# Four small moves in the program order of an FFT and MLP kernel: stage 4 behind the second product, a matrix load split elsewhere, one spectrum a step sooner, no product between two evictions

## The chip, the cores and the metric

The kernel runs on one core of a Trainium2 chip. The metric is the device time of one execution in microseconds (us), and smaller is better.

Short names: PE is the tensor engine, DVE the vector engine, ACT the scalar engine, POOL the GpSimd engine, SP the engine whose queue issues most transfers. L305 is line 305 of the kernel.

## The reference, cut to what matters

```python
def _attn_ref(x, filt_r, filt_i):                  # x: 8 x 3136 x 256
    X = np.fft.rfft(x, axis=1)
    F = (filt_r + 1j * filt_i)[None, :, :]
    return np.fft.irfft(X * F, n=x.shape[1], axis=1)

def _moe_ref(x, U, V, w_ch1, w_ch2):               # takes the result above as x
    xt = x.transpose(0, 2, 1)
    h = xt @ U @ V                                 # rank 32 over the sequence
    u = x + h.transpose(0, 2, 1)
    ch = np.maximum(u @ w_ch1, 0.0) @ w_ch2        # 256 -> 1024 -> 256
    return u + ch
```

The sequence of 3136 is transformed as 64 x 49, so the Fourier part is a row of small matrix products: stages 1 and 2 forward, a product with the filter, stages 3 and 4 back.

## The kernel before: the parts that matter

The program order of every engine is written by hand. For each of the 8 images:

- stage 1 (L305) into PSUM bank 4, copied out by ACT or DVE (`asb`, L309) and stored to memory (L313); its last rows are a tile of their own, `al`, stored at L297;
- stage 2 (L400) from the reloaded tiles `a` (L363) into banks 5 and 6; the filter products on DVE (L727 to L731) or POOL;
- stage 3 (L392) into bank 7, copied out by ACT (`esb`, L370) and stored (L377);
- stage 4 (L589) from the reloaded tiles `e` (L549) and the constant matrix `sv` into bank 4 again, evicted by DVE into `ut` (L594).

Then come the first product (L600, banks 0 and 1, with relu on ACT into `hring`, L604) and the second (L633, banks 2 and 3), the residual (L609), an eviction to `och` (L641) and the output store (L648).

The work on 512 tokens is a group. There are 52 groups of 8 steps, 416 steps with one relu each. I write (n, t) for step t of group n. The main loop:

```python
of = {"m": (0, 1), "o": (2, 3), "w": (4,), "e": (7,), ... "u": (5, 6)}[tag]   # PSUM banks by use

def st1(b, by=()):
    tag = "u" if b == 1 else "w"          # stage 1 of images 2 and up: bank 4, as stage 4

for n, gr in enumerate(groups):
    for t in range(8):
        for f, a in early[8 * n + t]:     # DVE and POOL products of the filter
            f(*a)
        mm1(gr, t)                        # first product, relu
        turns = {0: (5, 6), 5: (6, 7), 12: (6, 7)}.get(n, (2, 6))
        if n + 1 < len(groups) and t in turns:
            stage4(groups[n + 1], turns.index(t))       # one half of the next group's stage 4
        if n:
            mm2_part(groups[n - 1], t)    # second product of the group before
        for f, a in plan[8 * n + t]:      # stages 1 to 3, loads, stores
            f(*a)
```

So every step is a first product, perhaps a half of stage 4, a second product, and perhaps some piece of stages 1 to 3 of a later image.

## Time and profile before

| | us |
|---|---|
| median of 3 runs | 557.28 (556.37 to 560.54) |
| span in the profiled run | 553.0, mean granted clock 0.996 |
| PE waits for the copy of stage 1's result (L589 <- ACT asb) | 4.4 in 13 places |
| PE waits for the matrix `sv` | 2.2 in 1 place |
| PE waits for L594's eviction (L589 and L600 <- DVE ut) | 1.9 and 1.4 |
| PE waits for `e` of image 1 (L589 <- DMA e) | 1.2 in 1 place |

PE is busy for 93% of the span, so what can be won is the sum of its short idle times. A row of waits says who released PE. It does not say that PE would have been sooner without that wait, because another one may stand right behind it. The lines themselves are in the prediction.

### The profile page before, as it was taken

How to read it: one execution, taken by the hardware profiler on the slowest of the kernel's cores; microseconds unless marked ns; L12 is line 12 of the kernel's file. 1: busy time of each engine (PE TensorE's matmuls, PEld its weight loads, DVE VectorE, ACT ScalarE, POOL GpSimd, SP SyncE). 2: the span in 40 equal slices, each digit the busy share in tenths (PEclk: the TensorE clock that was granted, in tenths of full speed). 3: DMA queues.
4: the chain of work that ended last, by engine and by line, in shares of the span. 5: the costliest groups of instructions: out<-in, count | busy, mean ns of one | idle time of the engine just before them, and what ended most of it. 6: DMA issues, size and time to landing. Idle time of an engine off the chain costs nothing.

```text
span 553.0 us, 11722 instructions
## 1 busy us (share of the span) xinstructions
PE 516.4 (93%) x4540; PEld 371.9 (67%) x4540; DVE 353.8 (64%) x410; ACT 374.3 (68%) x677; POOL 291.6 (53%) x208
## 2 busy tenths in 40 slices
PE   5897789988989899999999999999999999999996
PEld 2644557666666576767776777777786777777775
DVE  7984747565456955768746775768646887543332
ACT  4655467746876578777777788668767677765663
POOL 6755277989873664834683185807563287300000
PEclk9999999999999899999999999999999999999999
DMA  9999895669663976974879459865654554343212
GB/s 195 166 194 188 197 221 152 173 189 232 167 184 104 211 198 150 234 214 120 195 204 215 128 168 243 164 202 152 181 163 131 140 161 121 107 113 115 96 77 86
DMA packets 85287, 91.96 MB, mean 166 GB/s; under 512 B 6725, under 2 KB 69464, under 8 KB 85232
## 3 DMA queue, kind: packets, MB, share of 16 engines
q1 hardware_dynamic: 67616, 75.02, 46.5%
q0 software_dynamic: 16912, 15.74, 18.7%
q8 instruction: 35, 0.57, 0.5%
q10 hardware_dynamic: 704, 0.46, 0.3%
q14 instruction: 20, 0.16, 0.1%
HBM read 57.12 MB, written 49.77 MB: 193 GB/s over the span
## 4 chain that ended last, share of the span: by engine, by line
PE 68%; DVE 9%; POOL 7%; DMA 5%; ACT 4%; issue 2%; SPq 0%; POOLq 0%; ACTq 0%; DVEq 0%
PE psum L633 24%; PE psum L600 23%; PE psum L400 5%; PE psum L392 4%; PE psum L589 4%; PE psum L609 3%; DMA x<-in_x_dram 2%; PE psum L305 2%; POOL fc L409 2%; DVE tb L729 2%; DVE tb L731 2%; POOL y L733 2%; ACT asb L309 1%; DVE ut L594 1%; DVE och L641 1%
## 5 line engine op out<-in xcount | busy, mean ns | idle before, releaser
L604 ACT ACTIVATE hring<-psum 128x512 f16<-128x512 f32 (+1 forms) x416 | 238.2, 576 | 113.4 <-PE psum L600 111.9
L600 PE MATMUL psum<-ut,w1sb 128*128 128x512 f16 (+1 forms) x832 | 240.3, 369 | 1.9 <-DVE ut L594 1.4
L633 PE MATMUL psum<-w2sb,hring 128*128 128x256 f16 x1536 | 230.7, 273 | 0.0
L733 POOL TENSOR_TENSOR y<-ta,tb 113x1024 f16<-113x1024 f16 x52 | 112.0, 2158 | 140.0 <-DVE tb L731 105.0
L633 PEld LDWEIGHTS <-hring 128*128 128x128 f16 x1536 | 143.0, 98 | 63.2 <-issue 3.0
L594 DVE CAST ut<-psum 128x512 f16<-128x512 f32 x94 | 69.6, 741 | 106.3 <-PE psum L589 81.3
L600 PEld LDWEIGHTS <-w1sb 128*128 128x128 f16 x832 | 104.4, 145 | 21.9 <-issue 5.5
L641 DVE COPY och<-psum 128x512 f32<-128x512 f32 x96 | 66.1, 689 | 50.2 <-PE psum L609 49.3
L370 ACT CAST esb<-psum 98x512 f16<-98x512 f32 x128 | 75.1, 587 | 25.4 <-PE psum L392 20.1
L589 PEld LDWEIGHTS <-e 96*128 96x128 f16 x752 | 34.5, 97 | 31.4 <-issue 11.9
L609 PE MATMUL psum<-idn,ut 128*128 128x128 f16 x392 | 54.1, 220 | 0.0
L309 ACT CAST asb<-psum 128x512 f16<-128x512 f32 x76 | 44.9, 590 | 13.3 <-PE psum L305 12.1
L727 DVE TENSOR_TENSOR ta<-psum,fb 113x1024 f16<-113x1024 f32 x37 | 45.0, 1217 | 6.2 <-PE psum L400 5.7
L589 PE MATMUL psum<-sv,e 96*128 96x64 f16 x752 | 37.4, 193 | 11.3 <-ACT asb L309 4.4
L729 DVE TENSOR_TENSOR tb<-psum,fc 49x1024 f16<-49x1024 f32 x37 | 45.4, 1226 | 1.0
L731 DVE TENSOR_TENSOR tb<-psum,fc 49x1024 f16<-49x1024 f32 x37 | 45.1, 1218 | 1.0
L609 PEld LDWEIGHTS <-ut 128*128 128x128 f16 x392 | 38.4, 98 | 4.9
L400 PE MATMUL psum<-a,w2t 98*128 98x512 f16 x120 | 36.2, 378 | 5.4 <-DVE tb L731 2.5
L727 POOL TENSOR_TENSOR ta<-pc,fb 113x1024 f16<-113x1024 f16 x15 | 32.4, 2161 | 13.4 <-ACT pc L737 13.4
L392 PE MATMUL psum<-y,g 113*98 113x512 f16 x98 | 37.6, 384 | 1.8 <-POOL y L733 0.9
L305 PE MATMUL psum<-x,wf 128*128 128x256 f16 x168 | 31.8, 272 | 3.2 <-DMA x<-in_x_dram 2.6
L187 POOL DMA_DIRECT2D x<-in_x_dram x48 | 31.0, 663 | 4.5 <-DMA w1sb<-in_moe_w_ch_dram 2.4
(112 smaller groups left out, 393.1 us busy)
## 6 DMA issues: line engine op xcount, KB each, us to landing
out_dram<-och SPq DMA_DIRECT2D x47, 512.0 KB
ct<-esb SPq DMA_DIRECT2D x64, 196.0 KB
x<-in_x_dram POOLq DMA_DIRECT2D x48, 256.0 KB, 7.6
e<-ct SPq DMA_DIRECT2D x46, 256.0 KB
a<-ct SPq DMA_DIRECT2D x56, 196.0 KB
ct<-asb SPq DMA_DIRECT2D x42, 256.0 KB
w1sb<-in_moe_w_ch_dram POOLq DMA_DIRECT2D x1, 512.0 KB, 6.6
w2sb<-in_moe_w_ch_dram POOLq DMA_DIRECT2D x1, 512.0 KB, 8.8
```

What stands on the lines that cost most here:

```text
L370: nc.scalar.copy(esb[b, k][:, 2 * half:2 * half + 2, :].rearrange("p s d -> p (s d)"), pe[0:98])
L392: nc.tensor.matmul(pe[0:98], g3[0:NZ, m, :], v, start=(n == 0), stop=(n == len(parts) - 1))
L400: nc.tensor.matmul(pz, w, a, start=True, stop=True)
L589: nc.tensor.matmul(pu[:, 64 * i:64 * i + 64], e2[b, c][:, i, 128 * dh:128 * dh + 128], sv[:, 64 * r:64 * r + 64], start=(i == 0), stop=Tru ...
L594: (nc.scalar.copy if gr is groups[0] and dh else nc.vector.tensor_copy)(o, v)
L600: nc.tensor.matmul(ph[:, 0:n], w1sb[:, dh, :, t], gr.ut[:, dh, 0:n], start=(dh == 0), stop=(dh == 1))
L604: nc.scalar.activation(h[:, 0:n], ph[:, 0:n], RELU)
L609: nc.tensor.matmul(o[:, dh * 128:dh * 128 + 128], gr.ut[:, dh, t0:t0 + n], idn, start=False, stop=(dh == 1), skip_group_check=True)
L633: nc.tensor.matmul(o, gr.h[tt][:, i * 128:(i + 1) * 128], w2sb[:, tt, :], start=(tt == 0), stop=False, skip_group_check=True)
L641: nc.vector.tensor_copy(gr.och[:, 2 * y:2 * y + 2, :].rearrange("p j d -> p (j d)"), gr.pc)
L727: eng.tensor_mul(ta, p[0:NZ], va)
L733: nc.gpsimd.tensor_add(ys[k], ta, tb)
```

## The change

It has four parts, each aimed at one of the rows above.

1. Where the step before ran a piece of stage 1 in bank 4, stage 4 goes behind the second product, which fills the time of the copy.
2. `sv` is split at column 1536 instead of 1024, so that stage 4 of blocks 0 to 2 needs only the first load.
3. The last two halves of stage 3 of image 1, and with them the loads of `e` for image 1 and its low-rank part, move up one step.
4. In groups 5 and 12 the DVE product that stood between the evictions of the two halves of stage 4 goes elsewhere.

```diff
-                    nc.sync.dma_start(sv[0:64, 0:1024], s4_d[:, 0:1024])
+                    nc.sync.dma_start(sv[0:64, 0:1536], s4_d[:, 0:1536])        # part 2
     def ok_dve(s):
-        return s % 8 not in (2, 6) and not small(s) and not small(s + 2)
+        return s % 8 not in ((6, 7) if s // 8 in (5, 12) else (2, 6)) and ...   # part 4 (cut)
-                    at(q + (3 if k == 7 else 2), three_q, k, half)
-            return 40
+                    at(q + 2, three_q, k, half)                                 # part 3
+            return 39
-    at(5, lambda: nc.sync.dma_start(sv[0:64, 1024:], s4_d[:, 1024:]))
+    at(5, lambda: nc.sync.dma_start(sv[0:64, 1536:], s4_d[:, 1536:]))           # part 2
-            if n + 1 < len(groups) and t in turns:
-                stage4(groups[n + 1], turns.index(t))
-            if n:
-                mm2_part(groups[n - 1], t)
+            behind = any(f is step1 for f, _ in plan[8 * n + t - 1])            # part 1
+            for side in (False, True):
+                if n + 1 < len(groups) and t in turns and behind == side:
+                    stage4(groups[n + 1], turns.index(t))
+                if n and not side:
+                    mm2_part(groups[n - 1], t)
```

More of the change, by code (lines that the diff above doesn't have):

```diff
@@ L696, in ok_dve @@
     def ok_dve(s):
-        return s % 8 not in (2, 6) and not small(s) and not small(s + 2)
+        return s % 8 not in ((6, 7) if s // 8 in (5, 12) else (2, 6)) and not small(s) and not small(s + 2)
     def step_at(w):
```

## The prediction

> **What bounds the kernel now.** I read the page first, then the waits of the tensor engine (PE), the timeline around each wait, the chain that ended last, and the windows of 20 us. From the page:
>
> ```profile
> PE 516.4 (93%) x4540; PEld 371.9 (67%) x4540; DVE 353.8 (64%) x410; ACT 374.3 (68%) x677; POOL 291.6 (53%) x208
> ...
> PE 68%; DVE 9%; POOL 7%; DMA 5%; ACT 4%; issue 2%; SPq 0%; POOLq 0%; ACTq 0%; DVEq 0%
> ```
>
> PE is the bound over the whole span, and from about 260 us on it is busy for 95 to 100% of nearly every window: little is to be won there, and whatever is won before is carried to the end. The waits of PE are short:
>
> ```profile
> PE psum L589 <- ACT asb L309: 4.4, 13, 0.7
> ...
> PE psum L589 <- DMA sv<-s: 2.2, 1, 2.2
> PE psum L589 <- DVE ut L594: 1.9, 1, 1.9
> ...
> PE psum L600 <- DVE ut L594: 1.4, 4, 0.4
> ...
> PE psum L589 <- DMA e<-ct: 1.2, 1, 1.2
> ```
>
> Columns: total us, times, longest. L589 is stage 4, L309 the copy of stage 1's result out of PSUM, L600 the first product. Each part of the change aims at one of these rows. The first row in the PE timeline (start, duration, idle in brackets):
>
> ```profile
> 85.31 0.38 PE L305 MATMUL psum<-x,wf 128*128 128x256 f16 x2
> 85.52 0.59 PE L600 MATMUL psum<-ut,w1sb 128*128 128x512 f16 x2
> 86.36 0.39 PE L589 MATMUL psum<-sv,e 96*128 96x64 f16 x8 [0.24 <-ACT asb L309]
> 86.59 0.60 PE L633 MATMUL psum<-w2sb,hring 128*128 128x256 f16 x4
> ```
>
> Stage 1 (L305) fills PSUM bank 4, ACT copies it out (0.59 us), stage 4 wants the same bank. The idle time in brackets understates the loss, since a busy bar holds the pipeline's tail too: two first products otherwise follow each other at 0.435 us, so stage 4 could have started at 85.52+0.435 = 85.955. It started 0.405 us later.
>
> Two stretches where PE is not what sets the pace. POOL and the load of x for image 3:
>
> ```profile
> 118.14 1.03 POOL L412 COPY fb<-fb 49x1024 f16<-49x1024 f16 x1
> 119.24 0.74 POOL L414 COPY fb<-fc 1x256 f16<-1x256 f16 x1
> 120.04 0.64 POOL L416 MEMSET fc<- 1x256 f16 x2
> 121.67 0.18 POOL L185 COPY x<-hring 1x1 f16<-1x1 f16 x1 [0.99 <-ACT hring L604]
> ```
>
> The chain that ended last runs over POOL without a break from 96.6 to 120.7 us, then the x load, and at 131.22 PE waits 0.44 us for that load. And DVE, where one product (L731) stands between the evictions of stage 4's two halves:
>
> ```profile
> 188.83 0.72 DVE L594 CAST ut<-psum 128x512 f16<-128x512 f32 x1
> 189.59 0.68 DVE L556 COPY e<-h 32x2048 f16<-32x2048 f16 x1
> 190.30 1.22 DVE L731 TENSOR_TENSOR tb<-psum,fc 49x1024 f16<-49x1024 f32 x1
> 191.55 0.73 DVE L594 CAST ut<-psum 128x512 f16<-128x512 f32 x1
> ```
>
> **What the Trainium skill says.** "TensorE: Matmul & The Clock Gate", section "Step-by-step: what each phase is for": matmuls stay in program order and only weight loads are pulled ahead. So products that do not need bank 4 can't pass a waiting stage 4 by themselves; the order in the program decides. The trace agrees: L633 follows L589 in every such place, though its inputs are old. "PSUM — Partial Sum Buffer", "PSUM bank collisions raise a hardware error": two engines may not touch a bank at once, so the wait for the copy can be filled but not dropped; here PE never starts before the 0.59 us copy ends. "DMA: Bandwidth & Descriptors", "Anatomy of one DMA": a fixed cost of about 2.0 us per transfer, mostly the receipt of the write. The trace agrees roughly: the last spectrum store of image 1 is issued at 110.44 (0.55 long) and the load that needs it follows at 113.53, 2.5 us later.
>
> **Part 1: stage 4 behind the second product.** By the order of the two programs 14 real halves move (groups 2, 3, 4, 7, 8, 10, 13, 14, 15). Their losses, each worked out as above, are 0.67, 0.41, 0.41, 0.42, 0.41 (80 to 106 us); 0.67, 0.40, 0.42, 0.82 (134 to 163 us); 0.40, 0.41, 0.71, 0.41, 0.40 (200 to 224 us): 6.9 us. Four L633 take 0.435 us, so each place gives at most 0.435: 5.8 us in sum. But stage 4 itself starts no sooner (it still waits for the copy), and so the eviction of stage 4 and the DVE products behind it come no sooner against stage 1. Where a stage 2 (L400) soon waits for those products, PE only waits there instead:
> - 80.5 and 86.4 count (0.84); 92.0 is lost, as the product before the L400 at 96.61 ends at 96.48, only 0.1 us of slack.
> - 98.1 and 105.6 count (0.82), up to the x load.
> - 134.0 is lost at the L400 at 138.44, which already waits 0.58 for DVE; of 139.9 and 146.0 some 0.38 is left at the L400 at 151.23; 162.5 is lost at the L400 at 166.25, which already waits 1.28.
> - 200.9 to 223.6: DVE has slack (for instance it ends 206.3 before an L400 at 207.5), all five count: 0.40+0.41+0.44+0.41+0.40 = 2.04.
>
> **Part 2: the stage-4 matrix in need's order.** Stage 4 of block 2 at 61.36 waits for the second part of sv, of which it reads the first 512 columns. Those now come with the first part, issued near 26 us. PE's loss is 61.36-(58.51+0.435) = 2.4 us. But its weight load waits for e until 60.68 (an idle of 2.02 us put down to DMA e). So the wait turns into one for e, and 0.6 us is won, not 2.4.
>
> **Part 3: spectrum 1 a step sooner.** The last two stage-3 halves, the load of e for image 1 and its low-rank part move up one step. Stage 4 at 117.39 waits 1.22 us (1.38 of issue) for that load. I expect the wait gone: with the SP queue in its new order the store goes out 1.5 to 2 us sooner. Two things take it back. First, the store of stage 1's last rows (al) now stands behind both e loads in the SP queue, and the load of the first spectrum block of image 2 waits for it: store about 112.5, landed some 2.5 us later, load 2.8 to 3.5 us, so at about 118.5 on the old scale while PE would be at its L400 (119.39 before) at 117.2. I expect a new wait of about 1 us there. Second, the x load for image 3 waits for POOL, which ends at 120.68 on the old scale. It was issued at 121.67, waiting for group 6's first relu. That relu can come sooner, the load by at most 0.97 us. So of 0.82+1.38+0.49 (the last is the wait at L600 at 120.54) only 0.97 arrives at 131.22.
>
> **Part 4: no product between the halves, groups 5 and 12.** In group 12 DVE's product of 1.23 us moves behind the second eviction. The first product's second half started at 192.34, could start at 191.62: 0.72 us. The wait of 1.9 us at 189.61 stays, because the products ahead of the first eviction stay. In group 5 no product stood between; nothing.
>
> **Sum:** before 96.6 us 0.6+0.84 = 1.45; to 131 us 0.97; to 166 us 0.38; at 192 us 0.72; to 224 us 2.04. Together 5.56 us of 557.28, which gives 551.7; I say 552.0.
>
> **Rivals.** (a) All PE losses named are won in full: 5.8 (part 1) + 2.4 + 1.4 + 0.7 + 0.5 = 10.8 us, 546.5. For it: PE carries 68% of the chain. Against it: DVE's waits at L400 (2.5 us in the waits) and the POOL stretch in the chain. (b) Nearly nothing comes through: the x load is not sooner because DMA is busy (shares of 0.93 to 0.95 in the windows around 60 to 80 and 120 to 140 us), stage 4 behind the products delays evictions and stage 1 waits for the bank in turn; 1 to 2 us, 555.5. Against it: the stretch from 200 to 224 us has slack on all engines. (c) Something turns worse: the delayed load of image 2's first block stalls PE by 3 us or more and pushes the later chain; 557 to 559. Against it: the x load wait behind it has room for 1 to 2 us. (d) The clock: from 190 to 193 us the windows show a granted clock of 0.50, behind the idle of 1.9 us. "TensorE: Matmul & The Clock Gate", "HAM oscillation — how this bites in real kernels", ties such drops to idle gaps of over about 3.4 us; this gap was shorter, so the trace does not quite agree. If new gaps move such a drop in or out, that is worth about 1.5 us either way.
>
> **Range and chances.** Terms of about 1 us are uncertain each (e's landing, the x load, the clock, the spread of the three runs from 556.4 to 560.5). I take 549.0 to 555.5. Faster by over 2% needs under 546.1, more than rival (a): 0.05. Slower by over 2% needs 568: 0.01. Within 2%: 0.94.
>
> **What would show it.** Right: the row L589 <- ACT asb falls from 4.4 us to under 1; L589 <- DMA sv gone and a wait for e of 1 to 2 us at the same place; L589 <- DMA e at 117 gone; L305 <- DMA x at 131 longer than 0.44, or a new L400 <- DMA a near 117; L400 <- DVE tb above 2.5. The gain by 131 us should be about 2.4 us and from 193 to 230 us about 2. Wrong: no new wait for x or a (then rival a is nearer), or L305 waiting for DVE ut in many steps (rival b).

## The result, and the profile after

The changed kernel took 551.04 us in the median of 4 runs (550.45 to 551.65), against 558.52 of 4 runs of the kernel before beside it (556.37 to 560.54). The ratio is 0.9867, with a 95% interval of 0.9822 to 0.9911: within 2%. Ratios here are the mean time of one kernel's fast runs over that of the other's of the same rounds, so not quite the ratio of the medians. In a later session the same kernel took 550.64 us against 555.12 (ratio 0.9905, 0.987 to 0.994). So the four runs of the kernel before in the first comparison lay at the high end of its spread, and some 5 us is the better figure for the gain: the mean of all 10 runs of the changed kernel is 550.8, that of 44 runs of the kernel before in four sessions 556.0.

The page of the changed kernel, busy time and chain:

```profile
PE 517.8 (94%) x4540; PEld 373.8 (68%) x4540; DVE 353.3 (64%) x410; ACT 374.1 (68%) x677; POOL 292.4 (53%) x208
...
PE 73%; DVE 9%; DMA 8%; POOL 4%; ACT 3%; issue 2%; SPq 0%; DVEq 0%; POOLq 0%; ACTq 0%
```

The same instructions and the same busy times, as it must be where only the order changes. In the chain PE has gone from 68 to 73% and POOL from 7 to 4%, but the transfers (DMA) from 5 to 8%: something new waits for a transfer. The waits of PE in the changed kernel (total us, times, longest):

```profile
PE psum L589 <- DMA e<-ct: 3.7, 3, 1.8
PE psum L400 <- DVE tb L731: 3.1, 4, 1.4
...
PE psum L589 <- DVE ut L594: 1.9, 1, 1.9
...
PE psum L392 <- ACT esb L370: 1.4, 3, 0.7
...
PE psum L600 <- DVE ut L594: 0.7, 2, 0.4
PE psum L400 <- DMA a<-ct: 0.7, 1, 0.7
...
PE psum L589 <- ACT asb L309: 0.5, 1, 0.5
```

The row of the copy fell from 4.4 us in 13 places to 0.5 in one. The row of `sv` is gone, and L600 <- DVE ut halved. But the wait for `e` grew from 1.2 us in one place to 3.7 in three, and L400 <- DMA a is new. What part 1 did is plain in the PE timeline, at the place that the prediction showed at 85.31 to 86.59:

```profile
84.95 0.59 PE L600 MATMUL psum<-ut,w1sb 128*128 128x512 f16 x2
85.38 0.60 PE L633 MATMUL psum<-w2sb,hring 128*128 128x256 f16 x4
85.82 0.40 PE L589 MATMUL psum<-sv,e 96*128 96x64 f16 x8
```

L600 and L633 follow each other at 0.43 us, then L589 at 0.44, with no idle. Before, L589 came 0.84 us behind L600.

To see which part won what, I cut each trace at the starts of the relus (one per step, so the same 416 marks in every kernel). Durations in us; "x late" marks where PE waited for the load of x for image 3, "w" a window of half clock, both explained below:

| kernel | (1,0) to (2,0) | (2,0) to (4,4) | (4,4) to (7,0) | (7,0) to (7,4) | (7,4) to (12,4) | (12,4) to (13,4) | (13,4) to (17,0) | (17,0) to the last relu |
|---|---|---|---|---|---|---|---|---|
| before | 11.21 | 33.53 | 28.24 | 6.53 x late | 48.33 | 12.93 w | 37.92 | 311.90 |
| before, again | 11.12 | 33.53 | 28.25 | 7.11 x late | 48.34 | 14.21 w | 37.91 | 311.93 |
| changed | 10.76 | 32.25 | 29.50 | 5.51 | 48.29 | 12.71 w | 36.19 | 311.91 |
| changed, again | 10.56 | 32.25 | 29.18 | 5.51 | 48.29 | 11.31 | 36.20 | 311.88 |
| part 1 alone | 13.07 w | 32.25 | 28.19 | 5.51 | 48.31 | 12.93 w | 36.28 | 311.90 |
| part 3 alone | 13.54 w | 33.53 | 29.44 | 5.92 | 48.33 | 14.82 w | 37.92 | 311.90 |
| parts 1, 2, 4 | 12.91 w | 32.24 | 28.19 | 6.36 x late | 48.29 | 11.31 | 36.20 | 311.91 |

Stretches without a mark, in kernels that have the same parts there, repeat within 0.1 us, except the first one and, with part 3, the one from (4,4), which repeat within 0.2 to 0.4 (the first one took 12.00 in experiment 7, where the wait for `sv` was 3.0 us instead of 2.2). That is much finer than the times of whole runs. Two places got better by over a microsecond, (2,0) to (4,4) and (13,4) to (17,0), and one got worse, (4,4) to (7,0). There image 1 takes over from image 0: part 3's place.

### The profile page after: what moved, and what is told of

Read it like the earlier page. It is cut to its first block, busy times and chain, and to the rows that moved or that the text cites. A ratio compares the mean times of both kernels' runs of the same rounds, so it can differ in the third digit from the quotient of the medians.

```text
span 549.9 us, 11727 instructions
## 1 busy us (share of the span) xinstructions
PE 517.8 (94%) x4540; PEld 373.8 (68%) x4540; DVE 353.3 (64%) x410; ACT 374.1 (68%) x677; POOL 292.4 (53%) x208
## 4 chain that ended last, share of the span: by engine, by line
PE 73%; DVE 9%; DMA 8%; POOL 4%; ACT 3%; issue 2%; SPq 0%; DVEq 0%; POOLq 0%; ACTq 0%
PE psum L633 26%; PE psum L600 25%; PE psum L400 5%; PE psum L392 4%; PE psum L589 4%; PE psum L609 3%; DMA e<-ct 3%; DMA x<-in_x_dram 3%; PE psum L305 3%; DVE tb L729 2%; DVE tb L731 2%; ACT esb L370 1%; DVE ut L594 1%; POOL y L733 1%; POOL x L187 1%
## 5 line engine op out<-in xcount | busy, mean ns | idle before, releaser
L600 PE MATMUL psum<-ut,w1sb 128*128 128x512 f16 (+1 forms) x832 | 240.5, 370 | 1.2 <-DVE ut L594 0.7
L633 PE MATMUL psum<-w2sb,hring 128*128 128x256 f16 x1536 | 230.7, 273 | 0.0
L633 PEld LDWEIGHTS <-hring 128*128 128x128 f16 x1536 | 144.0, 98 | 64.9 <-issue 2.5
L600 PEld LDWEIGHTS <-w1sb 128*128 128x128 f16 x832 | 104.1, 145 | 22.4 <-issue 5.5
L589 PEld LDWEIGHTS <-e 96*128 96x128 f16 x752 | 34.3, 97 | 25.1 <-issue 6.0
L731 DVE TENSOR_TENSOR tb<-psum,fc 49x1024 f16<-49x1024 f32 x37 | 45.1, 1218 | 1.0
L589 PE MATMUL psum<-sv,e 96*128 96x64 f16 x752 | 37.4, 192 | 7.9 <-DMA e<-ct 3.7
L400 PE MATMUL psum<-a,w2t 98*128 98x512 f16 x120 | 36.7, 382 | 6.1 <-DVE tb L731 3.1
L392 PE MATMUL psum<-y,g 113*98 113x512 f16 x98 | 37.7, 384 | 1.9 <-POOL y L733 0.9
```

The costliest lines, as they stand in the source:

```text
L392: nc.tensor.matmul(pe[0:98], g3[0:NZ, m, :], v, start=(n == 0), stop=(n == len(parts) - 1))
L400: nc.tensor.matmul(pz, w, a, start=True, stop=True)
L589: nc.tensor.matmul(pu[:, 64 * i:64 * i + 64], e2[b, c][:, i, 128 * dh:128 * dh + 128], sv[:, 64 * r:64 * r + 64], start=(i == 0), stop=Tru ...
L600: nc.tensor.matmul(ph[:, 0:n], w1sb[:, dh, :, t], gr.ut[:, dh, 0:n], start=(dh == 0), stop=(dh == 1))
L633: nc.tensor.matmul(o, gr.h[tt][:, i * 128:(i + 1) * 128], w2sb[:, tt, :], start=(tt == 0), stop=False, skip_group_check=True)
```

## The experiments

All kernels gave the right result. Four chips, each with 11 runs of the kernel before. Unless it is said, a kernel had 6 runs and its ratio is to the kernel before of its own call.

**1. The kernel before, again.** No edit. It says what a difference must exceed.

> The kernel before, unchanged, for a second trace and for the noise. The two profiled runs differ by 3.2 us (554.8 and 551.7), the timed medians by 7.5 us (558.5 and 551.0). Theory A: the profiled run of before was a lucky one, and its other runs lose 2 to 5 us more in one place that varies from run to run; then a second trace, if slower than 554.8, shows that place as a step in the times of the first-product relus. Theory B: the gap is only the profiler or the chip; then this trace agrees with the first within 0.5 us at every step. Ratio 0.998 to 1.002 in both.

557.05 us against 555.3 of the identical kernel (ratio 1.0022, 0.999 to 1.0054). Two sets of runs of one kernel differ by 1.7 us in their medians, so a part worth under 1 us can't be read from the times. The second trace is 2.8 us longer than the first, in three places as theory A has it: 1.0 before (1,0), 0.6 at the wait for x and 1.3 in the stretch with the half-clock window.

**2. Part 1 alone** (against the kernel before):

```diff
+            behind = any(f is step1 for f, _ in plan[8 * n + t - 1])
+            for side in (False, True):
+                ... stage4 where behind == side; mm2_part where not side
```

> Part 1 alone (stage 4 behind the second product). My prediction's steps give 0.84 + 0.82 + 0.38 + 2.04 = 4.1 us less than before in the trace, with the row L589 <- ACT asb falling from 4.4 us to under 1. Rival a (all PE losses are won): 5.8 us less. If the timed gain of the whole change (7.5 us) comes from part 1 alone, 6 us or more less in the times.

552.38 us, ratio 0.9941 (0.9907 to 0.9975): 3.3 us. By the table: 1.28 from (2,0) to (4,4), nothing in the next stretch, 1.64 from (13,4) to (17,0). From (7,0) to (7,4) it is 0.41 better than the 5.92 of part 3 alone, which has no wait for x there either. That is 3.3 to 3.5 us. Part 1 makes most of the gain of the change, some 3.3 of about 5 us; the prediction's steps gave 4.1.

**3. The change without part 3** (against the changed kernel):

```diff
-                    at(q + 2, three_q, k, half)
-            return 39
+                    at(q + (3 if k == 7 else 2), three_q, k, half)
+            return 40
```

> All but part 3 (spectrum 1 keeps its step). From the trace of the changed kernel, part 3 makes four waits (L392 <- ACT esb 0.67, L589 <- DMA e 0.84 left over, L400 <- DMA a 0.73, L589 <- DMA e 1.07) and its lead falls from 1.4 us at group 4 to 0.2 us at group 7. Theory A (part 3 costs more than it gives): 0.5 to 1.5 us faster than the changed kernel. Theory B (my prediction's step: part 3 gives up to 0.97 us): 0.5 to 1 us slower.

549.92 us, ratio 0.9894 (0.9855 to 0.9934). The changed kernel took 550.64 with 0.9905 in another session; the intervals overlap, so the times alone don't tell the two apart. The stretch (4,4) to (7,0) is 28.19 here, and 29.18 to 29.50 with part 3: part 3 costs 1.0 to 1.3 us there. In this trace image 3's x was late again (6.36), so up to (7,4) only 0.1 to 0.5 us of that cost is left against it.

**4. The store of `al` ahead of the loads** (against the changed kernel). In step (4,7) the piece of stage 1 with the store of `al` goes first, the loads of `e` after it.

```diff
+    plan[39].sort(key=lambda fa: fa[0] is not step1)
```

> The changed kernel with the last rows' store of stage 1 of image 2 put ahead of the two e loads in the SP queue. If that store behind the loads makes the new waits, L400 <- DMA a (0.73) and L589 <- DMA e (1.07) go and the kernel is 0.5 to 1.5 us faster than the changed one; the wait L392 <- ACT esb (0.67) stays. If the x load for image 3 sets the pace there, as I predicted, the wait moves to L305 <- DMA x and the gain is under 0.3 us.

549.66 us in the median of its five fast runs, ratio 0.9883 (0.9848 to 0.9918). Its profile fell in the slow state (clock 0.986), so I use only its stretch from (4,4) to (7,0), which holds no half-clock window: 29.09 us. Of the 0.5 to 1.5 us only 0.1 to 0.4 came in that stretch; the times of two sessions can't settle it. The new waits for `a` and for the second `e` are gone, but the wait for the first `e` is longer, 1.25 instead of 0.84 us, and L600 waits 0.73 for `ut` behind it. Their order in the queue only shares the loss out.

**5. Part 2 alone** (against the kernel before; 4 runs): the two lines of `sv` in the diff above.

> Part 2 alone (1536 columns of sv first). My prediction: the wait L589 <- DMA sv (2.2 us) turns into a wait for e of about 1.6 us at the same place, 0.6 us won there and carried to the end. In the two traces that hold part 2 so far the wait for e was 1.8 and 2.3 us. Theory A: e's landing sets the place, gain 0 to 0.6 us at step 2 of group 1 against step 0. Theory B: the wait is removed, 2.4 us won. In the times nothing beyond the noise of 2 us between runs.

557.14 us, ratio 0.9998 (0.9957 to 1.0039): nothing to be seen in the times. In the trace (1,0) to (2,0) is 10.33 us, and it is 10.56 and 10.76 in the changed kernel, against 11.21 and 11.12: 0.4 to 0.9 us. The wait for `sv` (2.2) is gone, and one for `e` stands at the same place, 1.36 us in this trace and 1.78 in the changed kernel's first.

**6. Part 3 alone** (against the kernel before; 4 runs): the three lines of part 3.

> Part 3 alone (spectrum 1 a step sooner). Theory A: it makes the waits L392 <- ACT esb (0.7), L400 <- DMA a and L589 <- DMA e behind it (0.5 to 1.1 each), so from group 4 to group 7 the kernel gains nothing or loses up to 1 us against before. My prediction's step: 0.5 to 1 us gained by group 7 (the wait for e of 1.2 us gone, limited by the x load).

558.61 us, ratio 1.0021 (0.998 to 1.0062). In the trace (4,4) to (7,0) is 29.44 us, 1.2 more than before, while the stretches on both sides of it are unchanged but for the wait for x. Part 3 alone makes its own stretch slower. The wait for x shrank at the same time (5.92 instead of 6.53 to 7.11).

**7. Part 4 alone** (against the kernel before; 4 runs): the line of `ok_dve`.

> Part 4 alone (no product between the halves in groups 5 and 12). Prediction: 0.7 us gained at step 0 of group 13 (the wait of L600 for DVE ut there gone), the wait of 1.9 us at L589 before it unchanged. Where a half-clock window of 3.4 us falls behind that wait, part of it is given back by step 4 of group 13.

555.46 us, ratio 0.9964 (0.9925 to 1.0004). (12,4) to (13,4) is 11.30 us here, as in the two other kernels with part 4 and no half-clock window at that place (11.31 each). In the changed kernel's first trace a window fell there: 12.71, hardly less than the 12.93 of before. Every trace without part 4 has a window there, so what part 4 gives at full clock was not measured.

**8. Another block of image 3 on POOL** (against parts 1, 2 and 4). In group 12 DVE's products stand ahead of the first eviction of stage 4, and PE waits 1.9 us for it. POOL takes block 1 of image 3 instead of block 2, which moves DVE's products away from there.

```diff
-        z = plan_mid(b, m, (2, 5) if b > 2 else (1, 3, 5))
+        z = plan_mid(b, m, (1, 5) if b == 3 else (2, 5) if b > 2 else (1, 3, 5))
```

> Parts 1, 2 and 4, and in image 3's spectrum block 1 goes to POOL in place of block 2, so that DVE has no product ahead of the first eviction of stage 4 in group 12. If the products ahead of that eviction make the 1.9 us wait of L589 for DVE ut, it falls under 0.3 us, and 1.6 to 2 us are won there against the version without part 3; and if that wait is what tips the clock to half near 190 us, no half-clock window stands there and the runs are 1 to 2 us faster again and less scattered. If the late e or the put_h copies make the wait, it stays over 1 us.

548.69 us (547.59 to 549.91), ratio 0.9852 (0.9817 to 0.9887). The wait of 1.9 us is gone, and (12,4) to (13,4) is 8.55 us, 2.8 less than the 11.31 of parts 1, 2 and 4. But (13,4) to (17,0) is 38.01 instead of 36.20, as POOL is now late for stage 3:

```profile
195.95 0.38 PE L392 MATMUL psum<-y,g 113*98 113x512 f16 x1 [1.50 <-POOL y L733]
```

With 0.4 more from (7,4) to (12,4), 2.2 of the 2.8 us are given back elsewhere. In another form, without DVE products in steps 4 to 7 of group 12, image 3's spectrum ended four steps later and its load no longer fitted: it did not build and was not run.

**9. The changed kernel, again.** No edit; for the same chip and rounds as the next two.

> The changed kernel, unchanged, beside the next two on one chip. In the runs so far the time lost to a lowered clock, (1 - mean granted clock) x time, was 4.0 and 4.7 us in the kernel before and 2.5 us in the changed one, and a run's time follows that loss with a slope near 1. Theory A (3 to 4 us of gain in the order of work, the rest is the clock's luck): ratio to before 0.989 to 0.994, and time less clock loss 3 to 4 us below that of before. Theory B (the whole 7.5 us belong to the change): ratio near 0.987 again.

550.64 us (549.13 to 551.65), ratio 0.9905 (0.987 to 0.994), as theory A has it. Less the clock loss its mean is 4.3 us below that of the kernel before in the same session. No half-clock window near group 12 in this trace.

**10. PE kept busy in the 1.9 us wait** (against the changed kernel), by eight products of constants into bank 7, whose result is overwritten:

```diff
+            if (n, t) == (12, 7):
+                keep_warm(8, psum[:, 7, :])
```

> The changed kernel with 8 products on zeros (1.7 us by their spacing of 0.216 us) put into the 1.9 us for which stage 4's second half waits in group 12; they write a bank that nothing reads. If the idle PE there is what tips the clock to half near 190 us, the half-clock window there is gone in the trace, the clock loss falls by 1 to 1.7 us on average, and the time by as much, though work was added. If the windows come independently of that wait, nothing falls and the kernel is 0 to 0.5 us slower.

550.89 us, ratio 0.9906 (0.987 to 0.9943): the same time. The mean clock loss is 1.9 us against 2.5, less than the 1 to 1.7 expected, and runs of one kernel scatter by more than 1 us in it. The trace shows no window at group 12, but the kernel it is compared with showed none there either in its second trace.

**11. Experiment 8 with `e` of image 0 one step sooner** (against experiment 8):

```diff
-    at(5, load_e2, 0, 2)
+    at(4, load_e2, 0, 2)
```

> The version with block 1 of image 3 on POOL (548.7 us median), and the load of e for block 2 one step sooner, so that in the SP queue it stands ahead of the two stores of 256 KB behind which it landed late. If those stores (about 2.6 us at some 200 GB/s) make e late, the wait L589 <- DMA e of 1.8 us at step 2 of group 1 falls to under 0.7 us, unless the x loads, which PE waits for just before, land later by the same amount: then L305 <- DMA x grows instead and nothing is won.

547.48 us (546.4 to 550.46), ratio 0.9865 (0.9824 to 0.9905): 7.6 us under the kernel before and 3.2 under the changed one on the same chip. It beats both and has the lowest median of all; by the ratios experiments 8 (0.9852) and 12 (0.987) can't be told from it. The wait of 1.8 us for `e` is gone, but its load now stands ahead of image 1's:

```profile
64.89 0.59 PE L400 MATMUL psum<-a,w2t 98*128 98x512 f16 x2 [1.14 <-DMA a<-ct]
```

(1,0) to (2,0) is 10.11 us, some 0.5 better than the 10.56 and 10.76 of the changed kernel.

**12. The output store out of the way** (against experiment 4). The question after experiments 4 and 6 was why `e` lands no sooner although it is asked for a step sooner. In the queue of SP a 512 KB output store stands right ahead of the spectrum store. Here the one output store of group 3 waits until step (5,1):

```diff
-                nc.sync.dma_start(dram(out.tensor, o, ...), gr.och)
+                store = (dram(out.tensor, o, ...), gr.och)
+                if gr is groups[3]:
+                    at(41, nc.sync.dma_start, *store)
+                else:
+                    nc.sync.dma_start(*store)
```

> The version with the last rows' store first, and also the 512 KB output store of group 3, which stood right ahead of image 1's last spectrum store in the SP queue, put behind the three spectrum loads of image 2. From the spectrum store's issue to the issue of the load of e that needs it took 3.1 us before, 3.5 to 3.8 us in the kernels with part 3. Theory A (that store's data stand ahead of it on the DMA engines): it falls to 2.5 us or less, the load of e goes out about 1 us sooner, the wait L589 <- DMA e of 0.8 to 1.3 us shrinks to under 0.4 us, and from step 4 of group 4 to step 0 of group 7 the kernel loses under 0.5 us, against 0.8 to 1.3 us in the kernels with part 3. Theory B (the receipt of the write alone takes that long): nothing moves.

548.09 us (546.74 to 549.73), ratio 0.987 (0.9842 to 0.9899). (4,4) to (7,0) is 26.84 us: 2.25 less than in experiment 4, 1.4 less than before, 2.3 to 2.7 less than changed. With the store out of the way the wait for image 1's first `e` is gone, which part 3 was meant to do. Whether the moved store would do as much without part 3 was not run. The queue of SP, first in the kernel before (start, length of the issue; L377 is the spectrum store, the first L549 the load that needs it):

```profile
108.43 0.98 SPq L648 DMA_DIRECT2D out_dram<-och  x1
109.50 0.55 SPq L297 DMA_DIRECT2D ct<-al  x1
110.44 0.55 SPq L377 DMA_DIRECT2D ct<-esb  x1
113.53 0.48 SPq L549 DMA_DIRECT2D e<-ct  x1
```

in the changed kernel:

```profile
107.87 0.57 SPq L648 DMA_DIRECT2D out_dram<-och  x1
108.54 0.53 SPq L377 DMA_DIRECT2D ct<-esb  x1
112.32 0.50 SPq L549 DMA_DIRECT2D e<-ct  x1
```

and here:

```profile
106.37 0.48 SPq L297 DMA_DIRECT2D ct<-al  x1
107.16 0.31 SPq L377 DMA_DIRECT2D ct<-esb  x1
109.69 0.49 SPq L549 DMA_DIRECT2D e<-ct  x1
```

From the spectrum store to the load is the time that the store takes to land: 3.09 us with the output store 2.0 us ahead, 3.78 with it 0.67 ahead, 2.53 with none ahead. (In the other traces with part 3 and the store 0.67 ahead it is 3.5 to 3.9.) The DMA packets in the traces show the same. In the changed kernel the output store's 128 packets of 4096 bytes run from 109.10 to 111.18, and 332 of the spectrum store's 392 packets of 512 bytes start only after the last of them has started; with part 3 alone all 392 do. In the changed kernel the spectrum store had moved up against the output store, and lost in the queue what it had won in time.

## Why the prediction was right or wrong

The prediction was 552.0 in a range of 549.0 to 555.5, and the kernel took 551.04 and 550.64 in two sessions. The total was right. Some of its terms were not, part 3's above all, and they and the clock happened to cancel. By its own terms, from the table above (a gain is positive; measured is the first trace of the kernel before less the changed kernel's first and second trace; the 0.41 of the place at 98.1 is moved out of the prediction's 0.97, where it was counted, to the stretch where it lies):

| term of the sum | predicted | measured |
|---|---|---|
| part 2 | 0.6 | 0.45, 0.65 |
| part 1 up to (4,4): the places at 80.5, 86.4 and 98.1 | 0.84 + 0.41 | 1.28, 1.28 |
| parts 1 and 3 from there to (7,4), where x is needed | 0.97 - 0.41 | -0.24, 0.08 |
| part 1, (7,4) to (12,4) | 0.38 | 0.04, 0.04 |
| part 4, (12,4) to (13,4) | 0.72 | 0.22 with a half-clock window, 1.62 without |
| part 1, (13,4) to (17,0) | 2.04 | 1.73, 1.72 |
| sum | 5.56 | 3.5, 5.4 |

**Part 1 was right, and so was most of its working.** Relu by relu, part 1 alone is ahead of the kernel before by 0.43 us behind the place at 80.5, by 0.81 behind 86.4 and by 1.18 behind 92.0. At the L400 that follows it falls back to 0.88, as the prediction said of the place at 92.0, and behind 98.1 it is at 1.28. The place at 105.6 was counted too. Its 0.39 us came (a lead of 1.67 at (4,7)) and outlasted the wait for `e`, which is 1.22 us long with part 1 and without. But at (6,0) 0.35 us was lost again: there the first product waits 0.68 us for `ut` instead of 0.33. DVE's copy ahead of that eviction ran longer, first before, then with part 1 alone:

```profile
118.59 1.13 DVE L556 COPY e<-h 32x2048 f16<-32x2048 f16 x1
```

```profile
117.98 1.48 DVE L556 COPY e<-h 32x2048 f16<-32x2048 f16 x1
```

At its shortest this copy takes 0.68 us. In 13 of the 14 traces a POOL instruction runs when it starts here, and in all 13 the copy ends 0.55 us after that instruction's end, whenever it began itself; in the 14th, experiment 12's, it takes 0.69. So POOL's pace seems to have set this place, which I had not seen and no run tested.

From (7,4) to (12,4) I kept 0.38 and 0.04 came: L400 <- DVE tb rose from 2.5 to 3.1 us, as expected, and took all of it rather than most. From (13,4) on 1.7 of 2.04 came. The general argument held: a wait that is filled is won only where nothing behind it waits for the same eviction.

**Part 2 was right.** A wait of 2.2 us removed, one of 1.78 for `e` behind it, and about half a microsecond won.

**Part 3 is the step that failed.** The prediction said: "I expect the wait gone: with the SP queue in its new order the store goes out 1.5 to 2 us sooner." Counted from the relu of (4,4), at 101.55 in the trace before and 100.13 in the one after, the spectrum store went out 8.89 us after it before and 8.41 in the changed kernel: 0.5 us sooner, not 1.5 to 2. It then took 3.78 us to land instead of 3.09, so the load was issued 12.19 after that relu instead of 11.98, later than before. The changed kernel's PE timeline:

```profile
105.54 0.59 PE L392 MATMUL psum<-uv,g 113*98 113x512 f16 x2 [0.67 <-ACT esb L370]
...
116.02 0.39 PE L589 MATMUL psum<-sv,e 96*128 96x64 f16 x8 [0.84 <-DMA e<-ct]
...
118.92 0.59 PE L400 MATMUL psum<-a,w2t 98*128 98x512 f16 x2 [0.73 <-DMA a<-ct]
...
122.87 0.41 PE L589 MATMUL psum<-sv,e 96*128 96x64 f16 x8 [1.07 <-DMA e<-ct]
```

Four waits, only the third of them foreseen. The first is a collision that part 3 makes: two halves of stage 3 now fall in one step, both need bank 7, and the second waits 0.67 us for ACT's copy of the first. That takes back part of what the store should have gained. The second is the old wait for `e`, still 0.84. The third is the wait for `a` behind the store of `al`, which the prediction put at about 1 us. The fourth stands behind the same store: PE reaches image 1's second block 1.07 us before its load lands. Experiment 12, against experiment 4, shows the cause that I had left out altogether, the 512 KB store ahead in the queue. With it out of the way, and `al` stored first, the wait for the first `e` and the wait for `a` are gone, and 0.23 us of the fourth is left. The bank collision of 0.67 us is still there, and the stretch is nevertheless 1.4 us shorter than before.

**The x load was wrong.** I expected it to set the pace there: its wait at 131 was to grow, unless a new one for `a` took up the time. The wait for `a` came, and the one for x vanished. The same piece of the chain before,

```profile
122.89 8.28 DMA x<-in_x_dram
```

and changed,

```profile
117.52 5.30 DMA e<-ct
```

show that the path to (7,4) led over image 3's x and now leads over image 1's second block of `e`. From (7,0) to (7,4) the changed kernel gains 1.0 us (6.53 to 5.51), which hides part 3's loss. This is no merit of the order alone: the wait for x makes 0.6 and 1.2 us in the two traces of the kernel before (their stretches less the 5.92 of part 3 alone), none with part 1 alone, and 0.85 with parts 1, 2 and 4 (less 5.51). It varies from run to run, and none of the kernels with part 3 showed it.

**Part 4 and the clock.** DVE's order is what was meant; in the changed kernel both evictions now stand ahead of the product, with `och` cut out ahead of L731:

```profile
187.60 0.73 DVE L594 CAST ut<-psum 128x512 f16<-128x512 f32 x1
188.36 0.68 DVE L556 COPY e<-h 32x2048 f16<-32x2048 f16 x1
189.07 0.74 DVE L594 CAST ut<-psum 128x512 f16<-128x512 f32 x1
...
190.41 1.22 DVE L731 TENSOR_TENSOR tb<-psum,fc 49x1024 f16<-49x1024 f32 x1
```

The gain is 0.22 us with a half-clock window in both traces. The 1.62 of the second trace holds the missing window too, and no trace without part 4 is free of it. The predicted 0.72 was mis-sized: it let the two halves of the first product start 0.22 us apart (191.40 and 191.62), as at full clock, but the trace is at half clock there, where the product before them takes 0.43 (L392 at 190.97, L600 at 191.40). So 0.51 was to be won at most. The same four microseconds in three traces (stretch, length, then PE, PEld, DVE, ACT and POOL busy with instructions begun, granted clock, DMA share, GB/s), before:

```profile
189.50:193.50 4.00, 3.58 (x22) 2.18 (x22) 3.26 (x5) 1.06 (x2) 1.96 (x2) 0.57 1.24 204
```

changed:

```profile
189.50:193.50 4.00, 4.00 (x23) 2.27 (x22) 2.09 (x3) 1.78 (x3) 1.73 (x1) 0.61 1.20 186
```

and parts 1, 2 and 4:

```profile
189.50:193.50 4.00, 3.90 (x35) 2.76 (x34) 3.21 (x4) 2.38 (x4) 1.36 (x1) 1.00 1.25 203
```

A busy PE is not a fast one: 23 instructions in 4.00 busy microseconds at a clock of 0.61, 35 in 3.90 at full clock. All three stand behind the same idle of 1.9 us ahead of stage 4's second half, which waits for the eviction of the first. The window costs 12.71 - 11.31 = 1.4 us, as rival (d) put it (1.5). It fell near group 12 in 5 of 5 traces without part 4, in 3 of 6 with part 4 and the idle, and in none of the three in which the idle was filled or gone (experiments 8, 10, 11). That fits the idle as its cause, but it is one or two traces of each kernel, and filling the idle (experiment 10) brought no time. Whether the idle tips the clock stays open.

The clock explains part of the total. Multiply one minus the mean granted clock of a run by its time, and take the mean over all runs: 3.8 us for the 44 of the kernel before, 2.5 for the 10 of the changed one. What remains is 552.2 and 548.3. So if a microsecond of lost clock costs a microsecond, then of the 5.2 us between the means 3.9 are the order of the work and 1.3 are less time at half clock, which the prediction had only as a risk either way. That slope is an assumption: among the runs of the kernel before it is 0.94 to 1.02 in three sessions and 0.39 in the fourth.

**The rivals.** (a), everything in full, 546.5: no, the gains stop at the DVE products and at the transfers, as expected. (b), 1 to 2 us: no, part 1's stretch from 200 to 230 us came nearly whole. (c), something turns worse: it did in part 3, by 1.0 to 1.3 us rather than 3. (d), the clock: such a window moved in and out, and it is worth 1.4 us. Two things stay open: the half-clock windows, and whether experiments 11 and 12 would add up, as they mend different stretches; together they were not run.

## What to carry to other kernels

Moving an instruction earlier in its own engine's order says nothing about when its data arrive: for each transfer that is to come sooner, look at what stands ahead of it in its queue and how large that is, and for each product that moves, at who else uses its PSUM bank in that step. When a change has several parts and each is worth less than the spread of the runs, cut the trace at instructions that all versions share and compare the stretches; here they repeat within 0.1 us where the times differ by 2. And a total that comes out right is no proof of its terms: here part 3's loss was offset by a wait for x that vanished and by less time at half clock.

## What the Trainium skill lacked or had wrong

- "DMA: Bandwidth & Descriptors", "Anatomy of one DMA — SWDGE (gpsimd) path": its fit of 2.0 us plus bytes over 436e3 gives an estimate of 2.46 us for the spectrum store of 196 KB. That fits a store with no output store ahead of it (2.53 us from its issue to the issue of the load behind it), though the section, which the prediction cites too, is about transfers issued from POOL, and this one goes out from SP. What the section lacks is a term for the queue: with a 512 KB store issued 0.67 us ahead the same store took 3.78 us, with it 2.0 us ahead 3.09. For the 512 KB the page's rate gives an estimate of 1.2 us; in the changed kernel's trace their packets take 2.1 us, so the page's rate would put the wait in the queue too low.
- "TensorE: Matmul & The Clock Gate", "HAM oscillation — how this bites in real kernels": it ties drops of the clock to idle gaps of over 3.4 us. Here drops to half clock, 3.4 us long in six traces and twice that in two, stood behind an idle of PE of only 1.9 us in 8 of 11 traces. The length agrees with the page, the threshold of that section does not fit, and what decides between a drop and none isn't in that section and was not settled by these runs.
- The same page, "Back-to-back issue gap": its sustained figure of about 131 ns for a product of N=512 isn't reached here. Two such products follow each other in 0.43 to 0.44 us in the densest stretches, 0.22 each, which is the page's figure for a single gap (216 ns).
